# A quarter of the attention steps multiply with v in float32, in a fixed pattern of engines, and x is turned on TensorE

## The chip, the cores and the metric

The kernel runs on one core of a Trainium2 chip. The metric is the device time of one execution in microseconds; lower is better. Of several runs of one kernel the median is given. A profile is one execution recorded on the chip; its span runs from the first to the last instruction of the program. The engines are named as in the profile: PE is TensorE (PEld its weight loads), DVE is VectorE, ACT is ScalarE, POOL is GpSimdE, SP is the engine that only issues DMAs. A "q" behind a name is the engine's queue of DMA issues.

## The reference

Block-sparse attention, and behind it a layer of eight experts of which each row uses two:

```python
scores = scale * np.matmul(q, k.transpose(0, 1, 3, 2))      # q, k, v: 4 x 8 heads x 768 x 64
mask = np.abs(blk_i - blk_j) <= 1                            # blocks of 32
mask = mask | (blk_i == 0) | (blk_j == 0) | (blk_i == n_blocks - 1) | (blk_j == n_blocks - 1)
...                                                          # and three sampled blocks per block of queries
scores = np.where(mask, scores, -1000000000.0)
scores = scores - np.max(scores, axis=-1, keepdims=True)
attn = np.exp(scores)
attn = attn / (np.sum(attn, axis=-1, keepdims=True) + 1e-09)
attn_out = np.matmul(attn, v)

x = attn_out.transpose(0, 2, 1, 3).reshape(B * S, H * D)     # 3072 x 512
noisy_logits = x @ w_gate + np.log1p(np.exp(x @ w_noise)) * noise
top2 = np.argpartition(-noisy_logits, 2, axis=1)[:, :2]      # weights by a softmax over the two
for e in range(8):                                           # w1: 512 x 1024, w2: 1024 x 512 each
    for k in range(2):
        mask = top2[:, k] == e
        out[mask] += top2_w[mask, k, None] * (np.maximum(x[mask] @ w1[e], 0.0) @ w2[e])
```

All inputs are float32. A row that is routed to another expert than the reference's is wrong as a whole, so the kernel keeps nearly float32 precision while it multiplies in 16 bits: it splits an operand into a high and a low part and adds three products.

## The kernel before

**Attention** goes over 32 heads (4 batches of 8), two heads to a group, so 16 groups. A head has six chunks of 128 keys; one chunk of one head is a step, and there are 192 steps, 12 to a group. `steps` (line 412) writes out the order of the work by hand: each engine executes its instructions in the order in which they are issued there. In step n:

- `exp(n, 0)` and `exp(n, 1)` (line 263): for each half of the queries two products on PE into a tile `pe` of PSUM (three buffers), and the exponential on ACT into `p32`, float32.
- `max_mm` and `max_red` (lines 212, 224) run 11 steps ahead: two products on PE into `pm` (two buffers), and the maximum over 768 keys. Either DVE reduces `pm` itself (line 239), or ACT copies it to bfloat16 (line 235) and DVE takes the maximum of the copy later (`max_copies`, line 247). `max_end` (line 249) scales a head's six maxima on DVE into a column of `qb`, from which the DMA transpose on SP's queue makes `q2`, the operand of the head's second product.
- `lo(n - 1)` (line 292): the high part of `p32` is the upper half of each float32, read in place; the low part `pl` is the difference, made on POOL (line 300) or on DVE (line 303).
- `av(n - 4)` (line 307): for each of six chunks of queries three products with v: high with high, high with low, low with high, 18 in a step, into `po` (one buffer for a head; its 65th column sums the weights).
- `av_end` (line 323) follows a head's last step: ACT copies `po` to `xo`, DVE takes the sums from `xo` (line 336), inverts and scales them, ACT makes the high part of x and POOL the low part.

Which engine takes a maximum or a low part is decided while the program is built: `work` adds up nominal durations for DVE, POOL and ACT in `busy`, and the engine that is behind gets the work; no step counts as shorter than STEP = 1480 ns. The loads of q, k and v of a group three ahead are issued on ACT's queue in a group's third step (`load`, line 146), and `SPLITAT` lists in which step of a group each part of the splitting of q, k and v is done (`split`, line 163).

**Routing.** When both heads of a group have their x, `rows` (line 525) sends it to DRAM and turns it by a DMA transpose, both on SP's queue. After four groups a batch is complete; `run` (line 536) is a generator that routes it in small pieces, a few turns in each step of attention. ZN and ZL are the turns that it waits before its first products (ZL in the last batch). It ends with writes into a table of slots on POOL's queue. The last batch is routed beside the first expert, 13 turns after each block of its first product.

**Experts.** Nine units (expert 0 in two parts) each gather their rows by the table, turn them by DMA, multiply twice in split float16, and add the weighted rows to the output by indirect DMA. The output was filled with zeros during attention, in eight writes of 768 KB on ACT's queue (`fill_out`, line 1053), one every four steps from step 20.

In `start`, ahead of the first step, the maxima of the first eight steps are taken; the second and fourth go by the copy.

## Time and profile before

| | us |
|---|---|
| median of three runs | 1049.55 |
| lowest and highest run | 1037.73, 1055.49 |
| span of the profiled execution | 1044.0 |
| attention, first exponential to the last copy of `po` | 25.6 to 448.4 |
| DVE busy over the whole span | 622.8 (60%) |
| ACT busy | 409.2 (39%) |
| POOL busy | 480.5 (46%) |

The profiled execution lies between the runs shown; its span leaves out what surrounds the program, so it is set beside the median by their distance of 5.5 us. The shares over the whole span mix two stages: up to 448 us attention, behind it the experts. The second section of the page shows that they are bound by different engines (40 slices of 26 us each; a digit is the busy share in tenths):

```profile
PE   2778777878778878889689999999999989999993
DVE  7999889999999999965314324234143242341220
ACT  2655556667657767633213213033032130330200
POOL 2666666767667758625335142250241422602211
DMA  8779996567577656585698739349186393581200
```

The change lies in the first stage and at the boundary of the two, in the first 18 slices. A busy PE there is not a PE at its peak, because the records of matmuls overlap.

### The profile page before, as it was taken

The page shows a single profiled execution, that of the slowest core. Times are in us where ns is not written, and L with a number is a line of the kernel's source. Part 1 is how long each engine was busy: PE and PEld are TensorE (multiplying, and loading weights), DVE is VectorE, ACT ScalarE, POOL GpSimd, SP SyncE. Part 2 cuts the span into 40 slices and gives each one's busy share as a digit, 9 for nine tenths or more (in the row PEclk, how much of TensorE's full clock was granted, in tenths as well). Part 3 has the DMA queues.
Part 4 walks back from the last instruction along what each step waited for, and adds up shares of the span by engine and source line. Part 5 has one row for each costly group of instructions (what it writes and reads, how often), then busy time and mean ns, then how long its engine had stood idle before and what let it go on. Part 6 is the DMA issues. An engine that isn't in the chain of part 4 may idle for free. (4 is left out here: it accounts for less than half of the span.)

```text
span 1044.0 us, 20814 instructions
## 1 busy us (share of the span) xinstructions
PE 889.1 (85%) x8413; PEld 533.5 (51%) x8413; DVE 622.8 (60%) x1024; ACT 409.2 (39%) x828; POOL 480.5 (46%) x480
## 2 busy tenths in 40 slices
PE   2778777878778878889689999999999989999993
PEld 1455555545555555565365555455455544554551
DVE  7999889999999999965314324234143242341220
ACT  2655556667657767633213213033032130330200
POOL 2666666767667758625335142250241422602211
PEclk9999999999899999999899999999999999999997
DMA  8779996567577656585698739349186393581200
GB/s 194 187 148 233 220 223 126 135 131 153 137 145 141 150 94 136 134 211 120 142 229 190 197 100 227 112 134 255 52 197 184 100 228 114 149 182 51 65 34 33
DMA packets 238075, 156.41 MB, mean 150 GB/s; under 512 B 172577, under 2 KB 213793, under 8 KB 237968
## 3 DMA queue, kind: packets, MB, share of 16 engines
q1 hardware_dynamic: 206816, 91.45, 43.1%
q0 software_dynamic: 14256, 39.58, 13.5%
q10 hardware_dynamic: 16896, 23.95, 8.0%
q8 instruction: 68, 1.11, 0.5%
q14 instruction: 39, 0.32, 0.1%
HBM read 79.62 MB, written 26.32 MB: 101 GB/s over the span
## 5 line engine op out<-in xcount | busy, mean ns | idle before, releaser
L274 ACT ACTIVATE p<-pe 128x384 f32<-128x384 f32 x384 | 180.5, 497 | 130.0 <-PE pe L273 103.0
L931 POOL DMA_INDIRECT out_dram<-y,mt x56 | 59.6, 1064 | 321.2 <-DVE y L929 216.2
L886 ACT ACTIVATE hh<-ph 128x408 f16<-128x408 f32 (+2 forms) x136 | 66.7, 491 | 333.5 <-PE ph L881 273.7
L220 PE MATMUL pm<-k,q 88*128 88x384 f16 x384 | 100.9, 349 | 78.1 <-DVE m L239 60.0
L300 POOL TENSOR_TENSOR pl<-p 128x768 f16<-128x768 f32 x89 | 142.2, 1605 | 47.7 <-ACT p L274 20.0
L887 DVE SCALAR_TENSOR_TENSOR hl<-ph,hh 128x408 f16<-128x408 f32 (+2 forms) x136 | 76.0, 560 | 128.5 <-ACT hh L886 128.5
L272 PE MATMUL pe<-q,k 128*128 128x384 f16 x384 | 130.6, 340 | 17.1 <-ACT p L274 12.4
L273 PE MATMUL pe<-q,k 128*128 128x384 f16 x384 | 130.3, 339 | 10.3 <-DMA q<-qb 10.3
L929 DVE SCALAR_TENSOR_TENSOR y<-py,mt,pv 128x512 f32<-128x512 f32 x48 | 36.0, 750 | 170.9 <-PE py L901 161.6
L320 PE MATMUL po<-vh,pl 128*128 128x65 f16 x1152 | 128.0, 198 | 5.3 <-DVE pl L303 5.2
L239 DVE TENSOR_REDUCE m<-pm 128x1 f32<-128x768 f32 x132 | 124.5, 948 | 13.5 <-PE pm L220 13.4
L316 PE MATMUL po<-vh,p 128*128 128x65 f16 x1152 | 128.5, 198 | 0.0
L318 PE MATMUL po<-vl,p 128*128 128x64 f16 x1152 | 128.2, 196 | 0.0
L303 DVE TENSOR_TENSOR pl<-p 128x768 f16<-128x768 f32 x103 | 127.3, 1243 | 0.0
L901 PEld LDWEIGHTS <-hh 128*128 128x128 f16 x768 | 74.9, 98 | 94.3 <-issue 8.1
L881 PE MATMUL ph<-xta,w1hb 128*128 128x408 f16 x512 | 110.6, 339 | 8.5 <-DVE hl L887 5.2
L316 PEld LDWEIGHTS <-p 128*128 128x128 bf16 x1152 | 110.6, 101 | 11.7 <-issue 1.5
L318 PEld LDWEIGHTS <-p 128*128 128x128 bf16 x1152 | 109.6, 102 | 11.8 <-issue 2.0
L320 PEld LDWEIGHTS <-pl 128*128 128x128 f16 x1152 | 109.2, 100 | 7.1 <-DVE pl L303 7.1
L220 PEld LDWEIGHTS <-q 88*128 88x128 f16 x384 | 39.2, 102 | 130.4 <-issue 102.2
L881 PE MATMUL ph<-xtb,w1ha 128*128 128x408 f16 (+1 forms) x448 | 92.8, 329 | 7.3 <-DVE hl L887 4.8
L881 PEld LDWEIGHTS <-w1ha 128*128 128x128 f16 x576 | 57.0, 99 | 43.9 <-issue 9.6
(175 smaller groups left out, 1763.3 us busy)
## 6 DMA issues: line engine op xcount, KB each, us to landing
wraw<-in_moe_w_dram SPq DMA_DIRECT2D x64, 512.0 KB, 5.9
q<-q SPq DMA_DIRECT2D x32, 192.0 KB, 5.9
raw_v<-in_v_dram ACTq DMA_DIRECT2D x16, 384.0 KB, 5.0
out_dram<-zero ACTq DMA_DIRECT2D x8, 768.0 KB, 6.1
x_rows<-x SPq DMA_DIRECT2D x16, 384.0 KB, 9.4
raw_k<-in_k_dram ACTq DMA_DIRECT2D x14, 384.0 KB
raw_q<-in_q_dram ACTq DMA_DIRECT2D x14, 384.0 KB, 12.0
k<-k SPq DMA_DIRECT2D x17, 192.0 KB
```

What stands on the lines that cost most here:

```text
L220: self.nc.tensor.matmul(pm[:, c, 0:384], r["q3"][0:K, h, t, :], r["k2"][0:K, h, 3 * c:3 * c + 3, :], start=True, stop=True)
L239: nc.vector.tensor_reduce(m, pm[:, :, 0:384], axis=AX.XY, op=ALU.max)
L272: nc.tensor.matmul(pe[:, 0:384], r["k1"][:, h, c, :], r["q1"][:, h, t, :], start=True, stop=False)
L273: nc.tensor.matmul(pe[:, 0:384], r["k2"][:, h, c, :], r["q2", h][:, t, :], start=False, stop=True)
L274: nc.scalar.activation(p32[:, t].rearrange("p t c -> p (t c)"), pe[:, 0:384], AF.Exp, scale=0.125)
L300: self.nc.gpsimd.tensor_sub(pl, p32, ph)
L303: self.nc.vector.tensor_sub(pl, p32, ph)
L316: nc.tensor.matmul(po[:, t, :], ph[:, t, :], r["vh"][:, h, c, :], start=(c == 0 and t == 0), stop=False, skip_group_check=True)
L318: nc.tensor.matmul(po[:, t, 0:D], ph[:, t, :], r["vl"][:, h, c, :], start=False, stop=False, skip_group_check=True)
L320: nc.tensor.matmul(po[:, t, :], pl[:, t, :], r["vh"][:, h, c, :], start=False, stop=(c == T - 1 and t == T - 1), skip_group_check=True)
L881: nc.tensor.matmul(ph[:, b, 0:m], w[wt][:, kb, fs], r["xt"][:, kb, a, o:o + m], start=i == 0, stop=i == last)
L887: nc.vector.scalar_tensor_tensor(self.hl[:, f, o:o + m], ph[:, b, 0:m], 0.0, hv, op0=ALU.max, op1=ALU.subtract)
```

## The change

- `LOW = "VFVPVFVPVFVP"` gives each of a group's 12 steps its way: V makes the low part on DVE, P on POOL (on DVE in the last 8 steps), and F has none. In an F step `av` multiplies the float32 `p32` with float32 v, six products in place of 18. The float32 v comes by three more loads of 32 KB a group (`vx`), and the exponential of these steps is scaled by 64, where the split steps have the 64 in v.
- The balance by nominal durations is gone. Every maximum is reduced on DVE from PSUM; the copies on ACT are gone. The column of `qb` is written by ACT instead of DVE.
- The sums of a head are read from `po` in PSUM, in the step of the copy; the scaling comes one step later, and x's low parts up to five steps later.
- x is turned by six transposes on PE for each of its two parts, through a buffer of `pe`; ACT copies the high part out, DVE the low part a step later. The DMA transposes of x are gone. ZN is 4 in place of 9, ZL 4 in place of 18.
- The zeros are written every 16 steps from step 24. The low parts of k and q have steps of their own in `SPLITAT`. TAIL is 8 in place of 12. Comments are removed.

```diff
-    TAIL = 12
+    TAIL = 8
...
-    SPLITAT = ((0, 0, 0), (1, 0, 1), (2, 1, 0), (5, 1, 1), (5, 2, None), (6, 3, None), (8, 4, None), (9, 5, None),
-               (6, 6, 0), (7, 6, 1), (7, 7, 0), (8, 7, 1))
+    SPLITAT = ((0, 0, 0), (1, 0, 1), (2, 8, 0), (2, 8, 1), (3, 1, 0), (4, 1, 1), (5, 2, None), (6, 3, None), (6, 9, 0),
+               (8, 4, None), (9, 5, None), (10, 9, 1), (7, 6, 0), (8, 6, 1), (9, 7, 0), (11, 7, 1))
+
+    LOW = "VFVPVFVPVFVP"
...
+        self.whole = [i for i, w in enumerate(self.LOW) if w == "F"]
...
+        self.vx = [self.natp.tile([P, len(self.whole), self.D + 1], F32, name=f"vx{i}") for i in range(4)]
+        for t in self.vx:
+            nc.gpsimd.memset(t[:, :, self.D:], 1.0 / VS)
+        self.up = self.natp.tile([P, 1], F32, name="up")
+        nc.gpsimd.memset(self.up, math.log(VS))
...
+            if nm == "v":
+                for j, i in enumerate(self.whole):
+                    h, c = divmod(i, self.T)
+                    (eng or self.nc.scalar).dma_start(
+                        self.vx[g % 4][:, j, 0:self.D],
+                        self.v[b, h0 + h].rearrange("(p t) d -> p t d", p=P)[:, c])
...
-        if copy is None:
-            copy = b["a"] + 691 <= b["v"] + self.ABIAS
-        if t < self.T - 1 and copy:
-            mc = self.sm.tile([P, 2, 384], BF16, name="mc", bufs=2)
-            nc.scalar.activation(mc, pm[:, :, 0:384], AF.Copy)
-            self.work(a=691, v=480)
-            self.copies.append((mc, m, self.now))
-        else:
-            nc.vector.tensor_reduce(m, pm[:, :, 0:384], axis=AX.XY, op=ALU.max)
-            self.work(v=870)
...
+        self.nc.vector.tensor_reduce(self.st[g]["m", h][:, t:t + 1], pm[:, :, 0:384], axis=AX.XY, op=ALU.max)
...
-            self.nc.vector.tensor_scalar(qb[:, h, :, 64 + self.NB], r["m", h], -1.0 / 64.0, LNS / 8.0,
-                                         op0=ALU.mult, op1=ALU.add)
+            self.nc.scalar.activation(qb[:, h, :, 64 + self.NB], r["m", h], AF.Copy, scale=-1.0 / 64.0, bias=LNS / 8.0)
...
-        nc.scalar.activation(p32[:, t].rearrange("p t c -> p (t c)"), pe[:, 0:384], AF.Exp, scale=0.125)
+        nc.scalar.activation(p32[:, t].rearrange("p t c -> p (t c)"), pe[:, 0:384], AF.Exp, scale=0.125,
+                             bias=self.up if self.low(n) == "F" else 0.0)
...
+    def low(self, n):
+        w = self.LOW[n % (self.G * self.T)]
+        return "V" if w == "P" and n >= self.NSTEP - self.TAIL else w
 
     def lo(self, n):
-        """The high part is the upper half of each float32, the low part what is left."""
+
+        if self.low(n) == "F":
+            return
...
-        if n < self.NSTEP - self.TAIL and b["p"] + 1764 <= b["v"] + 869 + self.PBIAS:
-            self.nc.gpsimd.tensor_sub(pl, p32, ph)
-            self.work(p=1764)
-        else:
-            self.nc.vector.tensor_sub(pl, p32, ph)
-            self.work(v=869)
+        (self.nc.gpsimd if self.low(n) == "P" else self.nc.vector).tensor_sub(pl, p32, ph)
         self.st["hl", n] = ph, pl
...
+        if self.low(n) == "F":
+            p32 = self.st.pop(("p", n))
+            x = self.vx[g % 4][:, self.whole.index(n % (self.G * T)), :]
+            for t in range(T):
+                nc.tensor.matmul(po[:, t, :], p32[:, t, :], x, start=(c == 0 and t == 0),
+                                 stop=(c == T - 1 and t == T - 1), skip_group_check=True)
+            return
...
-            nc.vector.tensor_scalar(r["rc", h], r["xo", h][:, :, D], 1e-9 * math.exp(LNS), None, op0=ALU.add)
+            po = r.pop(("o", h))
+            nc.vector.tensor_scalar(r["rc", h], po[:, :, D], 1e-9 * math.exp(LNS), None, op0=ALU.add)
...
-            self.av_end(j - 1, "sum", on_group)
-            self.max_copies(n - 1)
...
+            self.av_end(j, "sum", on_group)
             self.av_end(j - 1, "inverse", on_group)
...
-            self.av_end(j - 1, "scale", on_group)
-            self.av_end(j - 4, "low", on_group)
+            self.av_end(j - 2, "scale", on_group)
+
+            for lag in (4, 7, 9):
+                if lag == (4 if j - lag >= NSTEP - GT else 7 if (j - lag) % GT >= self.T else 9):
+                    self.av_end(j - lag, "low", on_group)
...
-    ZN, ZL = 9, 18
+    ZN, ZL = 4, 4
...
-    def rows(self, g, x):
+    def rows(self, g, x, ps, part):
...
-        nc.sync.dma_start_transpose(out=self.xT[:, kb].rearrange("p t a c -> p (t a) c"),
-                                    in_=x.rearrange("p t a c -> p (t a c)"))
...
+        pt = ps().bitcast(F16)[:, 0:T * P].rearrange("p (t c) -> p t c", t=T)
+        for t in range(T):
+            nc.tensor.transpose(pt[:, t], x[:, t, part], self.ident16)
+        if part == 0:
+            nc.scalar.activation(self.xT[:, kb, part], pt, AF.Copy)
+        else:
+            nc.vector.tensor_copy(self.xT[:, kb, part], pt)
...
     for i in range(8):
-        at(20 + 4 * i, fill_out, i)
+        at(24 + 16 * i, fill_out, i)
```

More of the change, by code (lines that the diff above doesn't have):

```diff
@@ L42 @@
     G = 2
-    ABIAS = 0
     XM = 2
@@ L387, in start @@
             self.max_mm(n)
-            self.max_red(n, n in (1, 3))
+            self.max_red(n)
             if n in (self.S0, self.S0 + 1):
                 self.split(1, n - self.S0)
+                for h in range(self.G):
+                    self.split(1, n - self.S0 + 8, h)
             if n == self.S0:
@@ L418, in steps @@
                 f()
-            for e in self.busy:
-                self.busy[e] = max(self.busy[e], n * self.STEP)
             if i == self.LOADAT and 4 <= g + 3 < self.NG:
@@ L556, in run @@
         nc.vector.tensor_copy(lc, pv)
-        work(v=325)
         yield
@@ L584, in run @@
         nc.vector.reciprocal(iw, w)
-        work(v=250)
         yield
@@ L1030, with on_group @@
     jobs = []
-    def on_group(g, x):
-        router.rows(g, x)
+    def on_group(g, x, part=0):
+        router.rows(g, x, psum[0], part)
+        if part == 0:
+            att.later(1, lambda: on_group(g, x, 1))
+            return
         b, kb = divmod(g, DM // P)
         if kb == DM // P - 1:
-            jobs.append(router.run(b, lambda: psum[0](), att.work))
+            jobs.append(router.run(b, lambda: psum[0]()))
     psum = [att.psum]
```

92 lines of the change are left out of this document (17 added, 75 removed).

## The prediction

> **What bounds the kernel now.** I read the table of busy time by stretch first, with cuts at the first exponential, after 60 steps, after 180 and at the end of attention; then the groups of instructions inside the two long stretches, the waits in them, and the timeline of TensorE.
>
> ```profile
> span 1044.0 us, 20814 instructions
> 25.60:157.70 132.10, 104.66 (x1377) 71.04 (x1375) 117.86 (x142) 76.70 (x175) 88.30 (x78) 0.94 0.96 203
> 157.70:428.40 270.70, 208.42 (x3047) 146.12 (x3045) 267.58 (x483) 181.95 (x402) 189.60 (x192) 0.95 0.65 135
> 25.60:157.70 132.10, 56.82 (x121) 0.94 0.96 203
> 157.70:428.40 270.70, 113.56 (x241) 0.95 0.65 135
> ```
>
> Each row has the stretch, its length and then busy time (and instructions) of PE, weight loads, DVE, ACT and POOL, the granted clock, the share of DMA and GB/s. The last two rows count line 274 alone, two exponentials to a step: 60 steps in the first stretch, 120 in the second, so five and ten groups of 12 steps. A group takes 26.4 us early and 27.1 us late. Late, VectorE is busy 267.6 of 270.7 us and sets the pace; early it is busy 117.9 of 132.1, and 14.2 us are lost to something else.
>
> ```profile
> 250.21 0.48 PE L220 MATMUL pm<-k,q 88*128 88x384 f16 x2 [1.39 <-DVE m L239]
> 250.54 0.33 PE L272 MATMUL pe<-q,k 128*128 128x384 f16 x1
> 250.86 0.19 PE L316 MATMUL po<-vh,p 128*128 128x65 f16 x1
> 251.37 0.20 PE L320 MATMUL po<-vh,pl 128*128 128x65 f16 x1
> 251.40 0.33 PE L272 MATMUL pe<-q,k 128*128 128x384 f16 x1
> PE pm L220 <- DVE m L239: 43.0, 34, 5.2
> ```
>
> TensorE is really used less than its busy time says: by starts, the two products of a maximum take 0.33 us (250.21 to 250.54), the two of an exponential 0.32 (to 250.86), and the 18 with v 0.54 (250.86 to 251.40, 0.03 each). A step is 0.33 + 2 x 0.32 + 0.54 = 1.51 us, a group 18.1 of 27. The last row, of the waits in the late stretch, shows what it waits for: VectorE's maxima.
>
> **The change, part by part.** First VectorE, late stretch (ten groups).
>
> ```profile
> L303 DVE TENSOR_TENSOR pl<-p 128x768 f16<-128x768 f32 x68 | 85.8, 1264 | 0.0
> L239 DVE TENSOR_REDUCE m<-pm 128x1 f32<-128x768 f32 x66 | 62.2, 947 | 1.0 <-PE pm L220 1.0
> L247 DVE TENSOR_SCALAR_CACHE_REDUCE junk<-mc 128x768 bf16<-128x768 bf16 x53 | 50.0, 944 | 0.6
> L257 DVE TENSOR_SCALAR qb<-m 128x6 f16<-128x6 f32 x20 | 15.0, 752 | 0.1
> L336 DVE TENSOR_SCALAR rc<-xo 128x6 f32<-128x6 f32 x20 | 9.1, 456 | 0.0
> L635 DVE TENSOR_SCALAR r_z<-r_ef 128x12 f32<-128x12 f32 x3 | 1.8, 586 | 0.0
> L668 DVE TENSOR_SCALAR r_cap<-r_z 128x12 f32<-128x12 f32 x3 | 0.8, 251 | 0.0
> L556 DVE COPY r_lc<-pe 128x192 f32<-128x192 f32 x3 | 1.0, 345 | 0.0
> L300 POOL TENSOR_TENSOR pl<-p 128x768 f16<-128x768 f32 x54 | 84.8, 1575 | 33.7 <-ACT p L274 13.3 <-PE po L320 7.7 <-PE pe L272 7.4
> L303 DVE TENSOR_TENSOR pl<-p x103: 910/951/2782, 32.5 to 445.9; 128x768 f16<-128x768 f32 x103
> L300 POOL TENSOR_TENSOR pl<-p x89: 1456/1467/2243, 29.5 to 427.8; 128x768 f16<-128x768 f32 x89
> 250.09 1.34 DVE L303 TENSOR_TENSOR pl<-p 128x768 f16<-128x768 f32 x1
> 251.35 0.16 DVE L336 TENSOR_SCALAR rc<-xo 128x6 f32<-128x6 f32 x1
> ```
>
> An instruction's record runs 0.08 us into the next one (250.09 + 1.34 ends at 251.43, the next starts at 251.35), so each costs its duration less 0.08.
> - Maxima: the copies on ScalarE (line 235) and VectorE's reads of them go; 54 more reductions come. -53 x 0.86 + 54 x 0.87 = +1. ScalarE is relieved, VectorE is not.
> - Low parts: all 192 steps have one now, 103 on VectorE and 89 on GpSimdE over the whole run. The fixed pattern has 6 V, 3 P and 3 F in 12 steps, and two P of the last 8 turn to V: 98, 46 and 48 without. So float32 mostly empties GpSimdE. Late, VectorE goes from 68 to 60. The late mean of 1.26 us beside a least of 0.91 and a median of 0.95, and 586 against 251 ns for two equally small operations, show VectorE held up beside GpSimdE. GpSimdE's share of the stretch falls from 70% (189.6 of 270.7) to some 62% (24 low parts of 1.58 us fewer, in about 246 us), so I take an eighth off the excess: 68 x 1.18 - 60 x 1.14 = -12. Bounds: -9 (no relief) and -28 (no excess left, 60 x 0.87).
> - The maximum's column (line 257) goes to ScalarE: -20 x 0.67 = -13. ScalarE pays some 0.2 us each, and waits in order for VectorE's last maximum; behind it stand the next step's exponentials, which TensorE has ready. GpSimdE and VectorE need those two steps later: hidden.
> - The sum (line 336) reads PSUM and no longer waits on a copy: 0.46 to about 0.17 us, the length of the undisturbed row at 251.35: -6.
> - Turning x: one copy of 768 values a group from PSUM. The reduction of 768 from PSUM takes 0.87; the copy of 192 took 0.27; between these, nearest the first: +9. Bounds +3 and +15.
> - Smaller operations, less held up: -3.
>
> Together -24 us of 270.7 (-45 to -10), if VectorE stays the bound.
>
> ```profile
> L239 DVE TENSOR_REDUCE m<-pm 128x1 f32<-128x768 f32 x58 | 54.8, 948 | 10.2 <-PE pm L220 10.1
> L303 DVE TENSOR_TENSOR pl<-p 128x768 f16<-128x768 f32 x23 | 27.6, 1199 | 0.0
> L257 DVE TENSOR_SCALAR qb<-m 128x6 f16<-128x6 f32 x10 | 8.9, 893 | 0.2
> L336 DVE TENSOR_SCALAR rc<-xo 128x6 f32<-128x6 f32 x9 | 6.2, 685 | 6.2 <-ACT xo L332 6.2
> PE pe L273 <- DMA q<-qb: 8.0, 3, 3.8
> L300 POOL TENSOR_TENSOR pl<-p 128x768 f16<-128x768 f32 x36 | 59.2, 1656 | 15.1 <-ACT p L274 6.7 <-PE po L320 5.4 <-PE pe L272 3.0
> ```
>
> Early (five groups) the same terms are: line 257 -8, line 336 -5, low parts 23 to 30 or +6, copies of x +3, operations held up less (GpSimdE loses 21 low parts of 36) -4: -8 on VectorE. Of its 14.2 us idle, 6.2 end on the copy of po, which the sum no longer needs, and 10.1 on TensorE, which itself waited 8.0 us for q2 by DMA. The eight 768 KB writes of zeros came every fourth step from 20 to 48; they now come every sixteenth from 24 to 136, and the 16 DMA transposes of x on SP's queue go. I give back 6 of the 14 us (0 to 12). Early: -14, bounds -20 and 0.
>
> TensorE's float32 products. No float32 matmul with 65 columns stands in the trace; the nearest rows are the float32 transposes of an expert's rows.
>
> ```profile
> 536.71 0.56 PEld L920 LDWEIGHTS pr<-r_ident,yt 128*96 128x96 f32 x4
> 536.92 0.60 PE L920 MATMUL pr<-r_ident,yt 128*96 128x128 f32 x4
> L920 PEld LDWEIGHTS pr<-r_ident,yt x32: 103/103/128, 536.7 to 1005.9; 128*48 128x48 f32 x28, 128*96 128x96 f32 x4
> L920 PE MATMUL pr<-r_ident,yt x32: 272/273/273, 536.9 to 1006.0; 128*48 128x128 f32 x28, 128*96 128x128 f32 x4
> 217.63 0.37 ACTq L152 DMA_DIRECT2D raw_k<-in_k_dram  x1
> ```
>
> Four take 0.60 us, the last one's 0.27 included: 0.11 apart for 128 columns, weight loads hidden. For 65 columns at that rate 6 products take 0.33 us a step. If nothing overlaps, load 0.13 and product 0.27, they take 6 x 0.40 = 2.4 us. I take 0.11 each, 0.66 us, as the row nearest in shape of the weights; against 0.54 now. TensorE's group becomes 12 x 0.97 + 9 x 0.54 + 3 x 0.66 + 12 transposes of x (0.055 each by the 0.16 for 384 columns) = 19.1 us; with 2.4 it is 24.4, as long as VectorE's group. So TensorE stays below VectorE at either bound, with no margin at the upper. The Trainium skill speaks against this. "FP8 and Floating Point Precision", section TensorE Precision Notes, has true float32 take four passes through the array, and "TensorE: Matmul & The Clock Gate", section LDWEIGHTS (loading the stationary operand), has a load take its columns / 1.2 ns, 107 for 128. If each pass had its own load ahead of it, a float32 step would cost 6 x 4 x (0.107 + 0.03) = 3.3 us (an estimate), TensorE's group 27.1, and the gains below would be gone: about 1050 us in place of my sum. The rows above show loads that hide behind the product ahead of them, in transposes; no float32 product in this trace can settle it.
>
> New waits, which the trace of before does not have. Three loads of 32 KB a group join ScalarE's queue: some 0.4 us of issue each (0.37 in the last row above), and the first waits for TensorE's last float32 product of the buffer's previous group, one step back; behind it stand a step's exponentials. The sum and, once a group, VectorE's copy of turned x hold po and one of three pe buffers until VectorE comes to them, so TensorE stands up to a VectorE step; VectorE then has a maximum and a low part queued, 1.7 us, against 1.2 us in which TensorE feeds the next. Bounds 0 and 1.5 us a group; I take 0.6 in 15 groups: +9. GpSimdE's key and query parts only move; x's low parts are later by up to 5 steps, before the routing needs them.
>
> Ends. Start: six maxima stand on VectorE alone and the column on ScalarE, worth about a step of a reduction, less the new memsets on GpSimdE: -1. Tail: 0. Boundary to the experts:
>
> ```profile
> L332 ACT ACTIVATE xo<-po x32: 486/491/521, 48.3 to 448.4; 128x390 f32<-128x390 f32 x32
> 451.53 1.42 SPq L531 DMA_TRANSPOSE r_xT<-x  x1
> 454.68 0.49 DVE L887 SCALAR_TENSOR_TENSOR hl<-ph,hh 128x320 f16<-128x320 f32 x1 [4.73 <-ACT hh L886]
> 472.54 0.48 DVE L887 SCALAR_TENSOR_TENSOR hl<-ph,hh 128x320 f16<-128x320 f32 x1
> PE py L901 <- DVE y L929: 5.7, 1, 5.7
> ```
>
> The last x was turned from 451.5 by DMA; now TensorE itself waits for it, about 3 us behind the last product (copied at 448.4), with the first expert's products queued behind. In return ZL drops from 18 turns to 4, one block of the first expert (13 turns; the two rows of line 887 are four blocks apart, 4.5 us each), and the 5.7 us in which a product waits for the last batch's slots shrink by that: -1, bounds -5 and +3. The experts are untouched.
>
> Sum: -24 - 14 + 9 - 1 - 1 = -31 on the profiled 1044.0, 1013. The median of the runs is 1049.55, 5.5 over that span; the same distance gives **1019 us**.
>
> **The rivals.** (a) *The waits eat it.* VectorE's low parts hardly fall in number (103 to 98). If the excess of 0.3 us does not fall with GpSimdE's load (late -18 in place of -24), early idle stays (-8) and the waits cost 1.2 us a group (+18), -10 is left: **1039 us**. For it: early VectorE is idle for reasons that the change touches only in part. Against it: late it is 99% busy and loses counted work. (b) *More than counted.* The excess vanishes (-45 late, -20 early with its idle time, waits 0): **985 us**. Against it: GpSimdE stays busy over half the time. (c) *TensorE becomes the bound, slower.* If each float32 product is made of four, each with a full weight load that does not hide, it costs 4 x (0.13 + 0.03) = 0.64 us by the rows above, a float32 step 3.8, TensorE's group 17.1 + 3 x 3.8 = 28.5 us. Against 26.4 early and 27.1 late that is 5 x 2.1 + 10 x 1.4 = +25: **1075 us**. It decides from 3.2 us a step, 0.53 a product. For it: nothing hides a load longer than the 0.03 us stream. Against it: the four float32 loads above did hide. The Trainium skill's "TensorE: Matmul & The Clock Gate", section Weight-path perf modes, names float32 as a type for which the fast weight load is off, which would speak for (c); no run here shows it.
>
> **How the numbers follow.** Forecast 0.57, own range 1003 to 1034; (a) 0.23; (b) 0.11; (c) 0.09. The range reaches into (a) and (b) to 992 and 1042. A measurement here can tell 2% from no change: below 1028.6 faster, above 1070.5 slower. Faster: most of the forecast (0.49), (b) 0.11 and a few of (a), 0.63. Slower: most of (c), 0.08. Same: 0.29.
>
> **What would show it.** Right: VectorE over 95% busy in the late stretch, groups of about 25 us; line 303's mean nearer 1.15; six float32 products start about 0.11 apart; no column or copy of maxima on VectorE; the long steps before 158 us fewer. Wrong: float32 starts 0.5 us apart and TensorE waiting for nothing; ScalarE waiting in its load issues or TensorE at po for the sum, with VectorE idle behind; or line 303 still at 1.26.

## The result and the profile after

The changed kernel takes 1071.76 us (median of 4 runs, 1067.49 to 1082.62), beside 1044.28 us (4 runs, 1037.73 to 1055.49) for the kernel before: a ratio of 1.029 with a 95% interval of 1.020 to 1.038. It is slower by about 3%, where 1019 us was predicted. Its profiled execution has a span of 1068.5 us, against 1044.0.

The busy time by stretch of the changed kernel, cut at the same events as before (first exponential, after 60 steps, after 180, and two rows more: to the end of the last copy of po, and to the end); the columns are those of the prediction:

```profile
span 1068.5 us, 20449 instructions
22.84:159.83 136.99, 114.74 (x1336) 83.00 (x1335) 102.50 (x138) 80.35 (x184) 56.98 (x56) 0.96 0.78 167
159.83:441.77 281.94, 239.20 (x2987) 179.12 (x2986) 233.30 (x416) 161.12 (x379) 151.99 (x169) 0.93 0.63 132
441.77:466.28 24.51, 21.22 (x328) 17.34 (x326) 15.54 (x19) 14.19 (x33) 10.69 (x10) 1.00 0.88 132
466.28:1068.50 602.22, 554.50 (x3652) 301.80 (x3652) 200.47 (x334) 131.58 (x214) 186.36 (x188) 0.97 0.54 140
```

The third busy number is VectorE. Late (the second row) its work fell from 267.6 to 233.3 us, and yet the stretch grew from 270.7 to 281.9: VectorE's idle time there went from 3.1 to 48.6 us. Every stretch but the start is longer. With 25.6, 132.1, 270.7, 20.5 and 595.1 us before, the differences are -2.8 (start), +4.9 (five early groups), +11.2 (ten late ones), +4.0 (the last) and +7.1 (the experts, with the boundary to them); together +24.5 with the rounding, the difference of the spans.

The groups of VectorE in the late stretch, with the idle time before them behind the second bar:

```profile
L233 DVE TENSOR_REDUCE m<-pm 128x1 f32<-128x768 f32 x120 | 113.0, 945 | 27.5 <-PE pm L226 27.5
L282 DVE TENSOR_TENSOR pl<-p 128x768 f16<-128x768 f32 x61 | 72.9, 1196 | 0.0
...
L524 DVE COPY r_xT<-pe 128x768 f16<-128x768 f16 x10 | 5.4, 541 | 0.0
...
L321 DVE TENSOR_SCALAR rc<-po 128x6 f32<-128x6 f32 x20 | 3.1, 157 | 17.6 <-ACT xo L317 17.6
```

The low part (1.20 us) and the sum (0.16) cost about what was predicted, the copy of turned x (0.54) less. The time is in the last column: 45 of the 48.6 us idle stand before maxima, ended by TensorE, and before the sum, ended by ScalarE's copy of po.

Who waited for whom in the same stretch (total us, times, longest):

```profile
ACT p L256 <- PE pe L255: 50.8, 58, 4.4
...
PE pe L254 <- ACT p L256: 28.2, 19, 4.9
ACT x L333 <- DVE xr L326: 27.5, 18, 4.3
DVE m L233 <- PE pm L226: 27.5, 23, 4.6
...
DVE rc L321 <- ACT xo L317: 17.6, 6, 5.1
...
ACT p L256 <- issue: 14.2, 5, 3.9
```

VectorE waits for TensorE, TensorE for ScalarE's exponentials, and ScalarE most of all for TensorE's products in turn. The row that no other engine explains is "issue": idle time in which ScalarE waited for nothing that the profile shows. One of its five places, first on ScalarE and its queue (ACTq), then on TensorE, then on VectorE, shows ScalarE's own DMA issues in it:

```profile
250.68 0.57 ACT L256 ACTIVATE p<-pe,up 128x384 f32<-128x384 f32 x1
250.85 0.42 ACTq L156 DMA_DIRECT2D raw_v<-in_v_dram  x1
251.15 0.52 ACT L181 ACTIVATE ka<-raw_k 128x384 f16<-128x384 f32 x1
251.32 4.17 ACTq L161 DMA_DIRECT2D vx<-in_v_dram  x3
255.59 1.25 ACT L256 ACTIVATE p<-pe 128x384 f32<-128x384 f32 x3 [3.93 <-issue]
```

```profile
253.31 0.49 PE L226 MATMUL pm<-k,q 88*128 88x384 f16 x2
256.14 0.32 PE L254 MATMUL pe<-q,k 128*128 128x384 f16 x1 [2.33 <-ACT p L256]
```

```profile
253.84 0.96 DVE L233 TENSOR_REDUCE m<-pm 128x1 f32<-128x768 f32 x1 [0.85 <-PE pm L226]
257.27 0.17 DVE L321 TENSOR_SCALAR rc<-po 128x6 f32<-128x6 f32 x1 [2.47 <-ACT xo L317]
```

The three loads of single columns of v hold ScalarE's sequencer from 251.32 to 255.49. The exponentials behind them start at 255.59, TensorE stands 2.33 us, the copy of po comes late, and VectorE stands 2.47 us before the sum. This is the line that the prediction named as the sign of being wrong: ScalarE waiting in its load issues, with VectorE idle behind.

The float32 products, by the timeline of TensorE and by the instructions of the tile po (duration in ns: least, median, most; first and last start):

```profile
249.63 1.45 PE L296 MATMUL po<-vx,p 128*128 128x65 f32 x12
250.92 0.33 PE L254 MATMUL pe<-q,k 128*128 128x384 f16 x1
```

```profile
L301 PE MATMUL po<-vh,p x864: 190/194/263, 38.9 to 465.5; 128*128 128x65 f16 x173
...
L296 PEld LDWEIGHTS po<-vx,p x576: 187/192/338, 41.8 to 464.3; 128*128 128x128 f32 x192
L296 PE MATMUL po<-vx,p x576: 217/275/457, 41.9 to 464.4; 128*128 128x65 f32 x192
```

The kernel has 6 x 48 = 288 float32 products, and the trace has 576 of them: each product is two load-and-multiply pairs. Twelve pairs, a step's six products, take 1.29 us (249.63 to 250.92), 0.11 apart, so a step costs 1.29 us on TensorE in place of 0.54. The Trainium skill, "FP8 and Floating Point Precision", section TensorE Precision Notes, gives true float32 four passes; the trace shows two records a product and cannot show what happens inside one.

### The profile page after: what moved, and what is told of

Its sections match the earlier page's. It is cut to its first block, busy times and chain, and to the rows that moved or that the text cites. A ratio compares the mean times of both kernels' runs of the same rounds, so it can differ in the third digit from the quotient of the medians.

```text
span 1068.5 us, 20449 instructions
## 1 busy us (share of the span) xinstructions
PE 936.9 (88%) x8317; PEld 583.7 (55%) x8317; DVE 568.2 (53%) x944; ACT 393.1 (37%) x816; POOL 413.5 (39%) x444
## 5 line engine op out<-in xcount | busy, mean ns | idle before, releaser
L233 DVE TENSOR_REDUCE m<-pm 128x1 f32<-128x768 f32 x192 | 180.5, 946 | 52.8 <-PE pm L226 52.6
L256 ACT ACTIVATE p<-pe 128x384 f32<-128x384 f32 x288 | 133.0, 493 | 105.6 <-PE pe L255 44.0
L282 POOL TENSOR_TENSOR pl<-p 128x768 f16<-128x768 f32 x46 | 82.4, 1790 | 150.1 <-ACT p L256 76.3
L226 PE MATMUL pm<-k,q 88*128 88x384 f16 x384 | 102.5, 353 | 25.7 <-DMA k<-kb 10.7
L282 DVE TENSOR_TENSOR pl<-p 128x768 f16<-128x768 f32 x98 | 116.5, 1189 | 1.9 <-ACT p L256 1.7
L305 PE MATMUL po<-vh,pl 128*128 128x65 f16 x864 | 96.8, 198 | 4.2 <-POOL pl L282 4.0
L301 PE MATMUL po<-vh,p 128*128 128x65 f16 x864 | 96.9, 199 | 2.1 <-DVE rc L321 1.9
L303 PE MATMUL po<-vl,p 128*128 128x64 f16 x864 | 96.7, 197 | 0.0
L301 PEld LDWEIGHTS <-p 128*128 128x128 bf16 x864 | 82.7, 101 | 15.3 <-DVE rc L321 7.6
L303 PEld LDWEIGHTS <-p 128*128 128x128 bf16 x864 | 82.1, 101 | 8.2 <-issue 2.2
L305 PEld LDWEIGHTS <-pl 128*128 128x128 f16 x864 | 82.0, 100 | 4.4 <-POOL pl L282 4.2
L841 PEld LDWEIGHTS <-w1hb 128*128 128x128 f16 x512 | 50.7, 99 | 54.6 <-issue 17.6
```

Source lines behind the costliest of these rows:

```text
L226: self.nc.tensor.matmul(pm[:, c, 0:384], r["q3"][0:K, h, t, :], r["k2"][0:K, h, 3 * c:3 * c + 3, :], start=True, stop=True)
L233: self.nc.vector.tensor_reduce(self.st[g]["m", h][:, t:t + 1], pm[:, :, 0:384], axis=AX.XY, op=ALU.max)
L256: nc.scalar.activation(p32[:, t].rearrange("p t c -> p (t c)"), pe[:, 0:384], AF.Exp, scale=0.125, bias=self.up if self.low(n) == "F" else ...
L282: (self.nc.gpsimd if self.low(n) == "P" else self.nc.vector).tensor_sub(pl, p32, ph)
L301: nc.tensor.matmul(po[:, t, :], ph[:, t, :], r["vh"][:, h, c, :], start=(c == 0 and t == 0), stop=False, skip_group_check=True)
L303: nc.tensor.matmul(po[:, t, 0:D], ph[:, t, :], r["vl"][:, h, c, :], start=False, stop=False, skip_group_check=True)
```

## The experiments

The kernel before took 1044 to 1094 us, by the chip and the time at which it ran, so each kernel is compared with runs of the kernel before that were made beside it. Two ratios from different rows can have been taken on different chips, and their difference is less sure than each ratio. All ratios, with their 95% intervals:

| kernel | median us | ratio | interval |
|---|---|---|---|
| changed kernel, first run | 1071.76 | 1.029 | 1.020 to 1.038 |
| changed kernel, again | 1107.60 | 1.023 | 1.018 to 1.028 |
| loads on SP's queue | 1100.78 | 1.011 | 1.002 to 1.020 |
| loads on GpSimdE's queue | 1073.82 | 0.990 | 0.986 to 0.995 |
| copies in place of the loads | 1067.37, again 1039.27 | 0.987, again 0.993 | 0.979 to 0.995, 0.990 to 0.996 |
| five buffers | 1106.88 | 1.018 | 1.009 to 1.027 |
| kernel before with the loads added | 1092.73 | 1.012 | 1.007 to 1.017 |
| scaling one step earlier | 1105.82 | 1.019 | 1.012 to 1.026 |
| no float32 products, no loads | 1099.55 | 1.013 | 1.006 to 1.020 |
| copies, sum as before | 1086.86 | 1.004 | 1.001 to 1.007 |
| copies, high part later | 1063.72 | 0.976 | 0.966 to 0.986 |
| copies, last 24 low parts on VectorE | 1067.96 | 0.982 | 0.970 to 0.993 |
| copies, old turns to wait | 1024.12 | 0.977 | 0.971 to 0.983 |
| copies, x turned by DMA | 1055.28, again 1019.71 | 0.969, again 0.974 | 0.960 to 0.978, 0.970 to 0.979 |
| copies, x by DMA, high part later | 1015.93 | 0.969 | 0.962 to 0.976 |
| loads kept, x turned by DMA | 1060.57 | 1.010 | 1.002 to 1.019 |
| no float32, no loads, x by DMA | 1061.16 | 1.009 | 1.005 to 1.013 |

**The loads: other queue, no loads, scaling, no float32.** The theories at this point were that the loads hold up ScalarE (1), that the scaling of x, now one step later, makes ScalarE wait (2), and that TensorE is the bound with the float32 products (3). The edits, each alone in the changed kernel:

```diff
-                    (eng or self.nc.scalar).dma_start(
+                    self.nc.sync.dma_start(
                         self.vx[g % 4][:, j, 0:self.D],
```

> The changed kernel with one edit: the three float32 loads of v a group are issued on SP's queue instead of ACT's. Theory 1 (the loads hold up ACT, whose late copy of po then holds up DVE): the 32 us that ACT's queue spends in them go, and the time falls by 15 to 30 us, to 1041 to 1056. Theory 2 (the scaling one step later makes ACT wait for DVE in front of x's high part): no more than 5 us less. Theory 3 (PE is the bound, by the float32 products): no more than 5 us less.

```diff
-            if nm == "v":
-                for j, i in enumerate(self.whole):
-                    h, c = divmod(i, self.T)
-                    (eng or self.nc.scalar).dma_start(
...
             nc.scalar.activation(r["vh"][:, hs, :, 0:D], vx[:, hs], AF.Copy, scale=VS)
+            for j, i in enumerate(self.whole):
+                hh, c = divmod(i, T)
+                if h is None or h == hh:
+                    nc.gpsimd.tensor_copy(self.vx[g % 4][:, j, 0:D], vx[:, hh, c])
```

> The changed kernel without the three loads: POOL copies float32 v out of the group's raw v when ACT makes its high part. Theory 1: 20 to 30 us less than the changed kernel, 1041 to 1051, and at least as good as the loads on SP's queue, because nothing waits in a queue of DMA issues. Theories 2 and 3: no more than 5 us less.

```diff
-            self.av_end(j - 2, "scale", on_group)
+            self.av_end(j - 1, "scale", on_group)
```

> The changed kernel with the scaling of x in the step where it stood before, one step earlier. Theory 2: the 38.7 us in which ACT waits for DVE's scaled x fall to the 12 of before, and the time by 15 to 25 us. Theory 1: ACT's waits move to its load issues, 0 to 5 us less.

```diff
-    LOW = "VFVPVFVPVFVP"
+    LOW = "VPVPVPVPVPVP"
```

> The changed kernel with no float32 step: F becomes P in the pattern (POOL makes 6 low parts a group), no loads of float32 v. By the changed kernel's trace a float32 step costs PE 12 products 0.11 us apart, 1.34 us against 0.54, 2.4 us a group. Theory 3: the time falls by 16 x 2.4 = 38 us, to about 1033, well below the kernel whose float32 v is copied. Theory 1: about the time of that kernel or a little more, 1041 to 1060, since the loads are gone in both and DVE meets POOL more often here.

In the run without float32 the tile of v keeps its three columns, which nothing reads. Copies in place of the loads give 0.987, 0.036 less than the 1.023 that the changed kernel takes when it is run again (below). Earlier scaling gives 1.019, hardly a difference: theory 2 does not explain the loss. Without the float32 products (and without the loads, since nothing reads them) the kernel takes 1.013, more than with the products and copies: theory 3 falls, since taking the products away makes it slower. On SP's queue the loads gain only 0.012, some 13 us, less than the 15 to 30 expected. The next four runs ask why.

**The loads by themselves, on a third queue, and the sum.**

> The changed kernel itself, to stand beside the others on the same chip. All theories: 1.02 to 1.04 of the kernel before, attention about 443 us.

The loads added to the kernel before:

```diff
             r[nm] = x.rearrange("p h (t d) -> p h t d", t=self.T)
+            if nm == "v":
+                for j, (h, c) in enumerate(((0, 1), (0, 5), (1, 3))):
+                    (eng or self.nc.scalar).dma_start(
+                        self.vx[g % 4][:, j, 0:self.D],
+                        self.v[b, h0 + h].rearrange("(p t) d -> p t d", p=P)[:, c])
```

> The kernel before, with the three 32 KB loads a group of single columns of v added on ScalarE's queue, into tiles that nothing reads. Nothing else is changed, so this is the price of the loads alone. Theory 1 (the loads make the changed kernel slow: ScalarE stands in their issues and the transfers on the shared DMA semaphores wait for one another): 1.02 to 1.05, since the same loads cost the changed kernel some 30 us. Rival theory 4 (the loads hurt only because the changed kernel's products must wait for them to land, or because they wait for TensorE to release the buffer): within 1% of the kernel before, since here nothing reads them.

The changed kernel's loads on GpSimdE's queue:

```diff
-                    (eng or self.nc.scalar).dma_start(
+                    self.nc.gpsimd.dma_start(
                         self.vx[g % 4][:, j, 0:self.D],
```

> The changed kernel with the same three loads a group issued on GpSimdE's queue, which has its own DMA semaphores in the trace (111 to 118, against 100 to 109 on SP and ScalarE). The bytes and the pieces are the same. Theory 1a (what costs is the place in the queues and the rotation of eight semaphores that SP and ScalarE share): attention falls to about that with copies in place of loads, 410 us, ratio 0.98 to 1.00, less what GpSimdE's issues cost. Theory 1b (what costs is the transfer itself, 256 bytes a piece, beside the other transfers): it stays near that with the loads on SP, 437 us, ratio 1.01 or more.

In the version with copies, the sum of the kernel before:

```diff
-            po = r.pop(("o", h))
-            nc.vector.tensor_scalar(r["rc", h], po[:, :, D], 1e-9 * math.exp(LNS), None, op0=ALU.add)
+            nc.vector.tensor_scalar(r["rc", h], r["xo", h][:, :, D], 1e-9 * math.exp(LNS), None, op0=ALU.add)
...
-            self.av_end(j, "sum", on_group)
+            self.av_end(j - 1, "sum", on_group)
```

> The changed kernel with copies on GpSimdE in place of the loads, and the sum again read from the copy of po one step later, as in the kernel before. With copies in place of loads VectorE still stood 17.5 us before the sum until ScalarE's copy of po ended. Theory 5 (the sum placed in the same step as the copy makes VectorE wait): 12 to 17 us less than with copies alone, ratio about 0.973. Rival (the wait only moves to the maxima, which wait for TensorE): no change beyond 0.5%, ratio 0.982 to 0.992.

The loads alone, read by nothing, make the kernel before 1.2% slower: they have a price of their own. It is a third of what they cost the changed kernel, and it lies between what theories 1 and 4 expected; why the changed kernel is hit harder stays open. On GpSimdE's queue, with the same bytes and pieces, the ratio is 0.990, 0.033 less than on ScalarE's beside the same runs. So the cost is the place in the queue and not the transfer. The issues of the loads in three kernels, changed, before with loads, and on GpSimdE, by the instructions of the tile vx:

```profile
L161 ACTq DMA_DIRECT2D vx<-in_v_dram x48: 334/522/1741, 17.9 to 363.8; - x48
```

```profile
L157 ACTq DMA_DIRECT2D vx<-in_v_dram x48: 334/477/1113, 16.7 to 354.5; - x48
```

```profile
L161 POOL DMA_DIRECT2D vx<-in_v_dram x48: 534/542/739, 18.8 to 337.9; - x48
...
  POOL vx L161: 35.7, 12
```

On ScalarE an issue takes 0.33 to 1.74 us; the 48 records of the changed kernel add up to 31.9 us, and the waits between them and the records ahead of them on ScalarE to 13.5. On GpSimdE the waits are longer still (the last row: 35.7 us for TensorE to release the buffer), and yet the kernel is faster. The Trainium skill, "DMA: Bandwidth & Descriptors", section Issuing engines are not separate DMA queues, says that another issuing engine saves only the sequencer's time, "usually small relative to the DMA itself". Here the other engine saves 0.033 of the kernel. Whether that is the sequencer's time alone, or also the rotation of semaphores told below, which GpSimdE's queue does not share (its transfers count on 111 to 118), this run does not separate.

About half of the loss lies at the start. By the starts of the exponentials, the first three groups take 90.6 us in the changed kernel and 90.6 with the loads on SP's queue, against 77.0 with them on GpSimdE's, 71.8 with copies (second run) and 79.1 in the kernel before. So SP's queue helps only behind these groups; what holds them up there was not settled.

The sum read from the copy of po a step later, as in the kernel before, is slower (1.004 with copies, against 0.987 and 0.993): the expectation was the other way. The sum behind ScalarE's copy waits visibly, and still the earlier place is the better one.

**What the issues wait for; what else is left with copies.** First the changed kernel with a fifth buffer:

```diff
-        self.vx = [self.natp.tile([P, len(self.whole), self.D + 1], F32, name=f"vx{i}") for i in range(4)]
+        self.vx = [self.natp.tile([P, len(self.whole), self.D + 1], F32, name=f"vx{i}") for i in range(5)]
...
-                        self.vx[g % 4][:, j, 0:self.D],
+                        self.vx[g % 5][:, j, 0:self.D],
```

> The changed kernel with five buffers for the float32 columns of v in place of four, the loads still on ScalarE's queue. In the changed kernel the third load of a group waits for TensorE's last float32 product on its buffer, 12 us in all; the 48 issues themselves take 32 us. Theory 1c (the wait for the buffer is what ScalarE hands on): ratio 0.99 to 1.005. Theory 1d (the issues themselves, and the waits for earlier transfers that use the same semaphore, are): at most 12 us better than the changed kernel, ratio 1.012 to 1.023.

Then three edits, each alone, in the version with copies:

```diff
-            self.av_end(j - 3, "high", on_group)
+            self.av_end(j - 4, "high", on_group)
```

> Copies on GpSimdE in place of the loads, and the high part of x one step later. With copies ScalarE still stood 44 us, 28 times, before the high part until VectorE had scaled x, with the second half of a step's exponentials queued behind. Theory 2b (this wait sets the length of the first step of a group, 3.7 us): 10 to 25 us less than with copies alone, ratio 0.965 to 0.978. Rival (the first step is long because VectorE has a low part, a scaling, a split of v and a maximum in a row; ScalarE only shows it): within 5 us, 0.982 to 0.992.

```diff
-    TAIL = 8
+    TAIL = 24
```

> Copies on GpSimdE in place of the loads, and the low parts of the last 24 steps on VectorE in place of the last 8. With copies the last two groups took 30.4 and 28.0 us, against 26.8 and 20.5 in the kernel before, with low parts on GpSimdE queued behind its scatters of slots and gathers of rows, and VectorE idle 7.4 us at the longest. Theory 6 (the fixed pattern costs where GpSimdE has other work): 5 to 12 us less, ratio 0.975 to 0.982. Rival: no change, 0.985 to 0.990.

```diff
-    ZN, ZL = 4, 4
+    ZN, ZL = 9, 18
...
+        nc.sync.dma_start_transpose(out=self.xT[:, kb].rearrange("p t a c -> p (t a) c"),
+                                    in_=x.rearrange("p t a c -> p (t a c)"))
-        pt = ps().bitcast(F16)[:, 0:T * P].rearrange("p (t c) -> p t c", t=T)
-        for t in range(T):
-            nc.tensor.transpose(pt[:, t], x[:, t, part], self.ident16)
...
```

> Copies on GpSimdE in place of the loads, and x turned by DMA again, with the turns to wait before the routing's products as in the kernel before. Prices the turn on TensorE: it costs ScalarE 0.8 us and VectorE 0.5 us a group and three stops of TensorE at the boundary to the experts, where the first product of the second layer came 38 us behind the last copy of po against 32. Theory 7 (the turn on TensorE costs the boundary 6 us and the groups little): 5 to 10 us less than with copies alone, ratio 0.977 to 0.982. Rival (the transposes on SP's queue hold up the others, as in the kernel before): 5 to 20 us more, ratio 0.991 to 1.005.

Five buffers give 1.018, within the interval of the changed kernel: the buffer's release is not what holds ScalarE, and the expectation had read these waits wrongly. The events of the trace, sorted by the semaphore that each transfer counts on, show what ends them. In this program the transfers of ScalarE's and SP's queues use eight semaphores in turn (100 to 104 and 107 to 109), and an issue waits until the transfer that had its semaphore last has landed. The longest wait of a third load in the late stretch, in both kernels:

```
kernel          issue at  wait us  semaphore  used last by
changed          200.79     2.50      108     SP's transpose q<-qb, issued at 193.00
five buffers     201.76     2.06      108     SP's transpose q<-qb, issued at 194.37
```

Before the third loads of all groups the waits add up to 12.2 us with four buffers and 12.0 with five, so it is not the buffer that they wait for. In the changed kernel four of the sixteen third loads wait 2.0 to 3.9 us, each until within 0.1 us of the landing of one of SP's transfers, three of them transposes that SP issued 7 to 8 us earlier; eleven of the others wait 0.1 us or less. The Trainium skill, "DMA: Bandwidth & Descriptors", section Why a DMA increments its semaphore by 16 and not by 1, says that of two transfers in flight on one semaphore, the later can fill the count of the earlier before that has landed; a wait ahead of the second use keeps them apart. The trace agrees so far as these issues start only behind that landing. The waits are the smaller part (13.5 us against 31.9 of issues); in the place shown at 251.32 there is none, and the three issues alone take 4.04 of the 4.17 us. Their sum is not the price on the path; that price is the 0.030 to 0.036 of the runs.

The high part one step later (0.976) and the low parts of the last 24 steps on VectorE (0.982) have intervals that reach that of the first run of copies alone, and no run of copies alone stands beside them: neither is settled. In the latter's profile the last two groups take 55.7 us, against 58.4 and 56.2 in the two profiles of copies alone; theory 6 expected 5 to 12 us less. With x turned by DMA the ratio is 0.969: the direction of theory 7, and more of it than expected.

**The second cause.** That edit undid two things, the turn on TensorE and the earlier start of the routing.

First the same edit in the changed kernel, with its loads:

> The changed kernel with x turned by DMA again and the turns to wait as before; the loads of single columns of v stay on ScalarE's queue. With copies in place of loads this edit took the ratio from 0.987 to 0.969. Theory 8 (the loads and the turn on TensorE each cost their own): 0.018 less than the changed kernel, 1.00 to 1.01. Rival (the transposes of x on SP wait for the loads on the semaphores that both queues share): no better than the changed kernel, 1.018 to 1.03.

Then, with copies and x still turned on TensorE, the turns to wait alone:

```diff
-    ZN, ZL = 4, 4
+    ZN, ZL = 9, 18
```

> Copies on GpSimdE in place of the loads, x turned on TensorE, but the turns to wait before the routing's first products as in the kernel before (9, and 18 in the last batch, in place of 4 and 4). Splits the edit before it. Theory 7a (the turn itself, its two copies and TensorE's waits cost the 19 us): 0.982 to 0.992, as with copies alone. Theory 7b (the routing that starts five turns earlier puts its VectorE operations where a group is full): 0.966 to 0.976, as with the DMA turn.

The next is the changed kernel with LOW = "VPVPVPVPVPVP", no loads, and the DMA turn:

> The changed kernel without the float32 steps (their low parts alternate between VectorE and GpSimdE, six a group each), without the loads, and with x turned by DMA. Beside copies with the DMA turn (0.969) it prices the float32 products themselves. Theory 9 (a float32 step takes a low part of 1.1 us from VectorE or 1.6 from GpSimdE, and costs TensorE 0.8 more): 0.98 to 1.00, that is 12 to 33 us slower. Rival (without loads the low parts on two engines do as well): 0.965 to 0.975.

The last of the four is copies, the DMA turn and the high part one step later:

> Copies in place of the loads, x turned by DMA, and the high part of x one step later: the parts that helped, together. Theory 2b (ScalarE's wait for the scaling sets the length of a group's first step, 4.3 us with the DMA turn): 0.957 to 0.964. Rival (the wait moves to the column of maxima, which then waited 59 us in place of 8): 0.966 to 0.972.

And two versions once more, on one chip:

> Copies on GpSimdE in place of the loads, nothing else, once more beside the version with the DMA turn on the same chip: 0.980 to 0.992.

> Copies in place of the loads and x turned by DMA with the turns to wait of the kernel before, once more: 0.964 to 0.975. If the two costs are real (theories 1 and 7), it stands 0.010 to 0.020 under copies alone on the same chip; if the difference between their first runs was between chips, within 0.005 of it.

Side by side on one chip, copies alone stand at 0.993 and copies with the DMA turn at 0.974: 0.019 apart, with intervals that do not meet. The old turns to wait alone, with x still turned on TensorE, give 0.977. That is 0.010 and 0.016 under the two runs of copies alone, both on other chips, so half or more of the second cost of 0.019 goes with the earlier start of the routing. The value lies between the two expectations, nearer to theory 7b. With the loads in place the DMA turn brings 1.023 to 1.010, with intervals that just touch: the two costs stand side by side. The first product of the second layer, by TensorE's timeline, in the kernel before, the changed one, and copies with the DMA turn:

```profile
480.93 0.38 PE L901 MATMUL py<-w2ha,hh 128*128 128x512 f16 x1
```

```profile
504.33 0.38 PE L861 MATMUL py<-w2ha,hh 128*128 128x512 f16 x1
```

```profile
459.85 0.38 PE L853 MATMUL py<-w2ha,hh 128*128 128x512 f16 x1
```

It comes 32.1 us behind the end of the last copy of po before (448.86), 38.1 after (466.28), and 32.1 again with the DMA turn (427.80). In the run with the old turns to wait and x on TensorE it was 34.4, so of these 6 us some 2.3 go with the turn and 3.6 with the earlier routing.

The busy time by stretch of copies alone (second run), then of copies with the DMA turn beside it, and the latter's waits for TensorE in the late stretch:

```profile
25.51:142.43 116.92, 109.10 (x1336) 80.34 (x1335) 103.99 (x138) 79.31 (x184) 62.64 (x74) 1.00 0.92 184
142.43:406.67 264.24, 232.62 (x2987) 175.37 (x2986) 234.19 (x416) 160.44 (x379) 158.21 (x196) 0.96 0.67 138
406.67:431.18 24.51, 21.21 (x328) 17.33 (x326) 15.54 (x19) 14.19 (x33) 10.69 (x10) 1.00 0.58 132
431.18:1036.40 605.22, 553.66 (x3652) 301.20 (x3652) 200.33 (x334) 131.59 (x214) 184.74 (x188) 0.97 0.56 139
```

```profile
25.31:141.44 116.13, 108.24 (x1292) 78.56 (x1291) 103.94 (x134) 76.20 (x181) 62.86 (x74) 0.99 0.97 194
141.44:404.68 263.24, 227.36 (x2867) 168.04 (x2866) 231.11 (x406) 153.90 (x367) 160.65 (x196) 0.95 0.79 156
404.68:427.80 23.12, 21.20 (x318) 17.03 (x317) 14.96 (x18) 13.37 (x31) 11.77 (x10) 1.00 0.84 144
427.80:1019.70 591.90, 551.00 (x3637) 300.24 (x3634) 200.14 (x333) 130.94 (x212) 186.46 (x188) 0.97 0.55 143
```

```profile
DVE m L231 <- PE pm L224: 29.6, 15, 5.6
```

Of the 16.8 us between the two spans only 3.2 lie in the groups (0.8, 1.0 and 1.4). The stretch behind the last copy of po differs by 13.3: 5.9 up to the product above (38.0 against 32.1) and 7.4 behind it. Whether these 7.4 belong to the edit is not shown, since the changed kernel and the kernel before, whose routing differs too, are only 1.1 us apart there.

With both costs removed the early groups take 116.1 us (132.1 before, 137.0 in the changed kernel), the late ones 263.2 (270.7 and 281.9). VectorE still idles 32 us late (263.2 less 231.1), nearly all of it before maxima that TensorE brings; TensorE is busy for 227.4 us there. So late VectorE is no longer the bound, even without the loads; what makes TensorE late there was not settled, and the other parts of the change (the zeros and the splitting in other steps, all maxima on VectorE) were not priced one by one.

Without float32, and else alike, the ratio is 1.009 against 0.974 and 0.969: the float32 steps, with the low parts that they save, are worth 0.035 to 0.040. Copies with the DMA turn, with or without the later high part (0.969), beat both kernels.

## Why the prediction was wrong

- **VectorE's work: right, and more of it than counted.** Its busy time was to fall by 24 us late and 8 early; it fell by 34 (267.6 to 233.3) and 15 (117.9 to 102.5). The low part on VectorE fell to 1.20 us (1.22 with the overlap), the sum to 0.16 (0.17); the copy of x, taken at 0.87, takes 0.46 (0.54 with the overlap). What failed is the condition, "if VectorE stays the bound": its idle time late grew by 45 us. Nor did it hold without the loads: with copies VectorE's busy time late is 33 us less than before, and the stretch only 6.5 us shorter.
- **The float32 price: too low.** 0.66 us a step was taken between 0.33 and 2.4; it is 1.29. TensorE's group rises from 19.1 to 21.0 us by that, under the 27.4 of an early group, and under the 23.2 of one with both causes removed. No run prices these 0.63 us by themselves. Rival (c), from 3.2 us a step, did not come about, and without the products the kernel is slower; that its 1075 us lie near the measured 1071.76 is chance.
- **The new waits: the step that failed.** Three loads of "some 0.4 us of issue each" on ScalarE's queue and the waits with them were put at 0.6 us a group, +9 in all, bounds 0 to 1.5 a group (+22). An issue takes 0.33 to 1.74, together 2.0 us a group, with 0.8 of waits, all in order ahead of a step's exponentials. The runs put the loads at 0.030 to 0.036 of the time, 31 to 38 us of 1050. The row from which 0.4 was taken is the shortest of three loads in a row; the two behind it in the trace take 0.49 and 0.48. The wait for the buffer, which the prediction named, hardly counts; the wait for a transfer on a shared semaphore was not in it. And the term was spread evenly over 15 groups, while some 19 us of the loss stand in the first three (90.6 against 71.8 with copies). The place shown at 251.32 has the waits handed on from ScalarE to TensorE and VectorE; how the issues and the semaphores share the loss stays open.
- **The boundary and the routing: wrong in sign.** Put at -1 (-5 to +3) because the last batch's turns to wait fell from 18 to 4. The last stretch is 7 us longer, and the earlier routing with the turn on TensorE costs 0.019 in all, some 20 us. A shorter wait before the routing was counted as a gain; the first product of the second layer came 6 us later instead, 3.6 of it with the earlier routing. Where the rest of the 20 us arises is open.
- **Early: near in sum, once the loads are gone; late: not.** -14 was predicted early; with copies and the DMA turn it is -16, but of other parts: VectorE's busy time falls by 14 in place of 8, its idle time by 2 in place of 6. Late the same kernel gains 7.5 in place of 24, the last group loses 3 and the experts gain 3 (its profile is from another chip than that of the kernel before).
- **Start and tail: small misses.** -2.8 for -1 at the start. The last group, put at 0, takes 4.0 us more.

Taken together: VectorE was relieved as predicted, but late that gave little time, and the waits of the loads and the earlier routing cost more than was gained. The version without the loads and with the old turn stands 29 us under the kernel before on its chip; that the sum said -31 is chance, since the sum holds the +9 of waits and VectorE's copies of turned x, which this version does not have, and late only 7.5 of the 24 came. Rival (a), the waits eat it, is nearest to what happened, at about three times the size that it was given: 31 to 38 us and some 20, where it had 18.

## What to carry to other kernels

A small load on the queue of an engine that feeds the path is priced by what stands behind its issue, not by its bytes. Here GpSimdE's queue, or copies of what is on the chip already, removed the loss; SP's queue removed only a third of it, so the other queue has to be tried. When an engine is relieved, ask which engine will set its pace next, before counting the relief as time. Count the transfers that share a rotation of semaphores: an added one can wait for another queue's transfer, as four of these loads did for 2.0 to 3.9 us.

## What was not expected of the hardware

- A float32 product of 65 columns is two load-and-multiply pairs in the trace, 0.11 us apart, against 0.03 for the same product in float16: 0.21 us (1.29 / 6) to 0.03. The records of its loads last 0.19 us, longer than the 0.11 from pair to pair, so they overlap with one another or with the products; which of the two sets the pace the trace does not show.
- VectorE's copy of 768 float16 values from PSUM takes 0.54 us, its reduction of 768 float32 values from PSUM 0.94.
- The issue of a 32 KB load with pieces of 256 bytes takes 0.33 to 1.74 us on ScalarE's queue (median 0.52) and 0.53 to 0.74 on GpSimdE's (median 0.54).
